# Pairing the output products of two slices beside attention, and moving a small load to another queue

## The chip, the core and the metric

The kernel runs on one core of a Trainium2 chip. The metric is the device time of one execution in microseconds (us). The core has a matmul engine (TensorE, PE; its weight loads appear as PEld), three engines for elementwise work (VectorE, DVE; ScalarE, ACT; GpSimd, POOL), SyncE (SP), which here only issues DMA transfers, and 16 DMA engines. PE writes its products to PSUM; DVE and ACT take them from there.

## What is computed

The reference, cut to what matters:

```python
# q, k, v: (4, 8, 576, 64); phi: (4, 8, 576, 32)
a = exp(phi - max(phi, axis=2)); a = a / (sum(a, axis=2) + 1e-9)
k_m, v_m = einsum('bhsm,bhsd->bhmd', a, k), einsum('bhsm,bhsd->bhmd', a, v)
attn = softmax(q @ k_m.T / sqrt(64))          # over 32 memory slots
x = (attn @ v_m).transpose(0, 2, 1, 3).reshape(2304, 512)
h = x @ w_in                                   # 512 -> 2048, weights in float64
x = (h * cos(h)) @ w_out                       # 2048 -> 512
p = domain_probs / (sum(domain_probs, -1) + 1e-9)
out = sum over 4 experts e of p[:, e] * (relu(x @ w1[e]) @ w2[e])   # 512 -> 1024 -> 512
```

## The kernel before

The kernel has three parts that overlap: attention, a first layer (h * cos(h)) and a second layer of four experts. Every fp32 product that has to be accurate is made of three matmuls on a high and a low half of both factors (`mm3`, L145 to L154; so nearly all matmuls have line L147), and the halves come from `split`: ACT writes the high half (L103), DVE or POOL the rest (L104).

**Attention** is eight parts, one for each of 4 batches and 2 groups of 4 heads. `attention` is a generator; a part is advanced by `next`. It loads phi, then k and v (two tiles of two heads, `kv`, three buffers) and q, all on SP's queue (L171, L178, L179, L182). The maximum `mx` (DVE, L189) goes through PE (`pt`, `bc`) and back (`bcs`), DVE subtracts (L201), ACT takes the Exp (L207). PE transposes q (`pq`, L214) and ACT copies it out (`qT`, L215). PE then forms `kvp` (L221), ACT scales it to `kvs` (L239), PE transposes that (`pkt`), DVE makes `kz` (L251) and `vz` (L257), and PE forms the scores `sc` (L271). DVE, POOL and ACT do the softmax (L278 to L293) and split the result into `attnT[b]`.

**The first layer** is worked in slices of 256 of the 2048 hidden columns (s = 0 to 7) for each batch b. A unit (s, b) has a projection, `vw = vz[b] x w_in slice` (`project`, L316: 16 matmuls into one PSUM buffer of pool `ps_o`, then a split into `vw`, two buffers), and, for each half `th` of the 576 rows, `hidden1` (12 matmuls `hp`, the h * cos(h) work and a split into `gt`, three buffers) and `output1` (L369): for each of four 128-row blocks d of the result, 6 matmuls into one PSUM bank `op`, and then a DVE instruction that copies the bank into the accumulator `acc` (slice 0, L384) or adds it (other slices, L386). Beside attention `op` takes its banks from `ps_o` alone, which has two buffers and which the projections use too; later it alternates between `ps_o` and `ps_a` (`wide`). `step1` works one unit: it calls `hidden1`, keeps up to two halves pending in `pend`, calls `output1` for the oldest one, and projects the next unit after the first half.

The order of the units is (0, 0), (1, 0), (0, 1), (1, 1), (0, 2), (1, 2), (0, 3), (1, 3) and then slice by slice over the batches. The first six are placed beside the attention parts 2 to 7, one unit for each part. The weights are float64 in memory; `narrow` (L122) loads them as `raw` and converts them with one ACT and three DVE instructions (L131, L132, L133, L136). The loads of the first slices' weights after the first one wait for a score Exp of attention on ACT's queue (`exps`, L285).

**The probabilities** are loaded and normalised by `load_probs` (L92): one transfer on POOL's queue, in pieces of 16 bytes (4 experts of one row), and four small DVE instructions.

The code is written in this order, but a scheduler reorders the instructions of each engine while the program is built; each engine then runs its own list strictly in order, and waits for others by semaphores. So what stands where is read from the built program.

Of the kernel before, what the change touches and what calls it, by code (L numbers as in the profile page):

```python
# [10 lines left out]
F32R = mybir.dt.float32r  # L11
# [13 lines left out]
def tile_kernel(  # L25
# [13 lines left out]
    nc = tc.nc  # L39
    B, H, S, D = q.shape  # L40
# [7 lines left out]
    TH = S // 2  # L48
    KD = DM // 128
    FS = 256  # L50
    NFC = FS // 128
    NS1 = DFF // FS
# [37 lines left out]
    p_all = const.tile([128, NT // 128, E], F32, name="p_all")  # L90

    def load_probs():  # L92
        nc.gpsimd.dma_start(out=p_all, in_=probs.rearrange("(i p) e -> p i e", p=128))
        p_sum = const.tile([128, NT // 128], F32, name="p_sum")
        nc.vector.tensor_reduce(out=p_sum, in_=p_all, axis=AX.X, op=ALU.add)
        nc.vector.tensor_scalar_add(p_sum, p_sum, 1e-9)
        nc.vector.reciprocal(out=p_sum, in_=p_sum)
        nc.vector.tensor_tensor(
            out=p_all, in0=p_all, in1=p_sum[:, :, None].to_broadcast([128, NT // 128, E]), op=ALU.mult
        )  # L100
# [44 lines left out]
    def mm3(ps, lt, rt, first, last, more=False):  # L145
        for i, (a, b) in enumerate(((0, 0), (0, 1), (1, 0))):
            nc.tensor.matmul(  # L147
                out=ps,
                lhsT=lt(a),
                rhs=rt(b),  # L150
                start=first and i == 0,
                stop=last and i == 2,
                skip_group_check=more,
            )  # L154
# [144 lines left out]
    wi = {}  # L299
    wo = {}  # L300
# [15 lines left out]
    def project(b, wi):  # L316
        vw_ps = ps_o.tile([128, 2, FS], F32, tag="o", name="vw_ps")
        for g in range(2):
            for i in range(HG):
                nc.tensor.matmul(  # L320
                    out=vw_ps[32 * i:32 * i + 32, g, :],
                    lhsT=vz[b][:, g, i, :],
                    rhs=wi[:, 2 * g + i // 2, :],
                    start=True,
                    stop=True,
                )
        vw = cs.tile([128, 2, 2, FS], F32R, tag="vw", name="vw")
        split(vw[:, 0], vw[:, 1], vw_ps)
        return vw

# [2 lines left out]
    def hidden1(b, th, vw):  # L333
        y_all = cs.tile([128, NFC, TH], F32, tag="y", name="y")
        kk_all = cs.tile([128, NFC, TH], F32, tag="kk", name="kk", bufs=1)
        gt = cs.tile([128, 2, NFC, TH], F32R, tag="g", name="gt", bufs=3)
        step = NFC if wide[0] else 1
        for f0 in range(0, NFC, step):
            hp = ps_h[0].tile([128, step, 512], F32, tag="h", name="hp")
            for i in range(step):  # L340
                fc = f0 + i
                for g in range(2):
                    mm3(
                        hp[:, i, :TH],
                        lambda x: vw[:, x, g, fc * 128:fc * 128 + 128],
                        lambda x: attnT[b][:, x, g, th * TH:th * TH + TH],
                        g == 0,
                        g == 1,
                    )
            hv = hp[:, :, :TH]  # L350
            y = y_all[:, f0:f0 + step]
            kk = kk_all[:, f0:f0 + step]
            marks.append(nc.scalar.activation(out=y, in_=hv, func=ACTF.Copy, scale=INV_2PI, bias=0.25))
            if wide[0]:
                nc.scalar.activation(out=kk, in_=y, func=ACTF.Copy, bias=ROUND)
                nc.vector.scalar_tensor_tensor(  # L356
                    out=y, in0=kk, scalar=ROUND, in1=y, op0=ALU.subtract, op1=ALU.subtract
                )
            else:
                nc.vector.tensor_scalar(  # L360
                    out=kk, in0=y, scalar1=ROUND, scalar2=ROUND, op0=ALU.add, op1=ALU.subtract
                )
                nc.gpsimd.tensor_tensor(out=y, in0=y, in1=kk, op=ALU.subtract)
            nc.scalar.activation(out=y, in_=y, func=ACTF.Sin, scale=-TWO_PI if wide[0] else TWO_PI)  # L364
            nc.vector.tensor_tensor(out=y, in0=hv, in1=y, op=ALU.mult)  # L365
            split(gt[:, 0, f0:f0 + step], gt[:, 1, f0:f0 + step], y, nc.gpsimd if wide[0] else nc.vector)
        return gt

    def output1(s, b, th, gt, wo):  # L369
        for d in range(KD):  # L370
            c = d % 2 if wide[0] else 0
            op = (ps_o, ps_a)[c].tile([128, 512], F32, tag="oa"[c], name="op")
            for fc in range(NFC):
                mm3(
                    op[:, :TH],
                    lambda x: wo[:, x, fc, d * 128:d * 128 + 128],
                    lambda x: gt[:, x, fc, :],
                    fc == 0,
                    fc == NFC - 1,
                )  # L380
            t0 = (b % 2) * S
            dst = x1v[:, b // 2, d, t0:t0 + S].rearrange("p (c u) -> p u c", u=2)[:, th]
            if s == 0:
                nc.vector.tensor_copy(out=dst, in_=op[:, :TH])  # L384
            else:
                nc.vector.tensor_tensor(out=dst, in0=op[:, :TH], in1=dst, op=ALU.add)  # L386

    vws = {}
    wide = [False]
    pend = []  # L390
    order = [(s, b) for b in range(B) for s in range(2)]
    order += [(s, b) for s in range(2, NS1) for b in range(B)]

    def project_next(n):
        if n + 1 < len(order):
            s2, b2 = order[n + 1]
            vws[n + 1] = project(b2, wi[s2])

    def step1(n):
        s, b = order[n]  # L400
        for th in range(2):
            if n > 8 and b in (1, 2) and s + 1 < NS1:
                (load_in, load_out)[b - 1](s + 1, marks[-1], th)
            pend.append((s, b, th, hidden1(b, th, vws[n]), wo[s]))
            if len(pend) > 2:
                output1(*pend.pop(0))
            if th == 0:
                project_next(n)

    parts = [attention(b, g) for b in range(B) for g in range(2)]  # L410
    np_ = len(parts)
# [13 lines left out]
        next(parts[i])  # L425
    load_in(1, exps[0])
    load_out(1, exps[1])
    nu = 0
    for n in range(2, np_):
        part = parts[n]  # L430
        if n + 2 < np_:
            next(parts[n + 2])
        if n + 1 < np_:
            next(parts[n + 1])
        if n + 2 < np_:
            next(parts[n + 2])
        next(part)
        next(part, None)
        if n <= 7:
            step1(nu)  # L440
            nu += 1
    wide[0] = True
    c_ctx.close()
    ps_h[0] = p_ctx.enter_context(tc.tile_pool(name="ps_h2", bufs=2, space=PSUM, reuse_waits="tile"))
    load_probs()
    at_ctx.close()
    wc = ctx.enter_context(tc.tile_pool(name="wc", bufs=2, side="right", reuse_waits="tile"))
    for n in range(nu, len(order)):
        s, b = order[n]
        if n == 6:  # L450
            load_in(2)
        if n == 8:
            load_out(2)
        step1(n)
    for p in pend:
        output1(*p)
    cs_ctx.close()

# [214 lines left out]
```

## Time and profile before

| | |
|---|---|
| three timed runs | 1221.29, 1222.03, 1224.94 us; median 1222.03 us |
| profiled execution | 1223.36 us, of which the span from the first to the last instruction is 1221.6 us |
| PE busy | 1181.9 us (97%), 7946 matmuls |
| DVE, ACT, POOL busy | 868.2, 485.6, 525.2 us |
| attention and the first six units | about 0 to 165 us |
| rest of the first layer | to about 454 us |
| second layer | about 454 us to the end |

All times of the trace count from the start of the span. Busy time is the union of an engine's instructions; matmuls overlap, so the share of a stretch in which PE is idle tells more than its busy share. The granted clock of PE has two levels in this trace, 1.0 (2.4 GHz) and 0.5 (1.2 GHz).

### The profile page before, as it was taken

How to read it: one execution, taken by the hardware profiler on the slowest of the kernel's cores; microseconds unless marked ns; L12 is line 12 of the kernel's file. 1: busy time of each engine (PE TensorE's matmuls, PEld its weight loads, DVE VectorE, ACT ScalarE, POOL GpSimd, SP SyncE). 2: the span in 40 equal slices, each digit the busy share in tenths (PEclk: the TensorE clock that was granted, in tenths of full speed). 3: DMA queues.
4: the chain of work that ended last, by engine and by line, in shares of the span. 5: the costliest groups of instructions: out<-in, count | busy, mean ns of one | idle time of the engine just before them, and what ended most of it. 6: DMA issues, size and time to landing. Idle time of an engine off the chain costs nothing.

```text
span 1221.6 us, 20025 instructions
## 1 busy us (share of the span) xinstructions
PE 1181.9 (97%) x7946; PEld 1050.3 (86%) x7946; DVE 868.2 (71%) x1571; ACT 485.6 (40%) x854; POOL 525.2 (43%) x609
## 2 busy tenths in 40 slices
PE   6788999999999999999999999999999999999998
PEld 5466788999999988888889898898889989888997
DVE  5798988798788788666666666678656665666665
ACT  2475755666566663232222223244222322322221
POOL 1443533332333852445445445546534544453420
PEclk8589999999999999999999999999999999999999
DMA  9953001112112110111111111113111111111102
GB/s 224 251 147 77 21 36 52 36 53 70 35 36 72 52 52 18 37 52 51 35 53 53 35 40 57 43 36 129 54 35 50 55 35 35 53 52 36 52 1 78
DMA packets 48062, 72.89 MB, mean 60 GB/s; under 512 B 2624, under 2 KB 31328, under 8 KB 47968
## 3 DMA queue, kind: packets, MB, share of 16 engines
q1 hardware_dynamic: 41024, 55.85, 16.1%
q10 hardware_dynamic: 6880, 15.73, 4.2%
q8 instruction: 62, 1.02, 0.3%
q14 instruction: 32, 0.26, 0.1%
q0 software_dynamic: 64, 0.04, 0.0%
HBM read 66.88 MB, written 4.72 MB: 59 GB/s over the span
## 4 chain that ended last, share of the span: by engine, by line
PE 62%; DVE 1%; issue 0%
PE op L147 33%; PE hp L147 29%; DVE x L485 1%; DVE sA L477 0%; DVE sB L498 0%; DVE acc L617 0%; DVE ht L582 0%; DVE u L558 0%; DVE acc L386 0%
## 5 line engine op out<-in xcount | busy, mean ns | idle before, releaser
L147 PE MATMUL op<-wb,ht 128*128 128x512 f32 x1728 | 439.3, 396 | 0.0
L147 PEld LDWEIGHTS hp<-x,wa 128*128 128x128 f32 x2688 | 380.3, 189 | 24.4 <-DVE x L485 3.6
L147 PE MATMUL hp<-x,wa 128*128 128x320 f32 (+1 forms) x2688 | 393.6, 295 | 3.2 <-DVE x L485 2.9
L147 PEld LDWEIGHTS op<-wb,ht 128*128 128x128 f32 x1728 | 312.7, 188 | 58.5
L617 DVE SCALAR_TENSOR_TENSOR acc<-op,p_all,acc 128x512 f32<-128x512 f32 x270 | 201.8, 748 | 137.7 <-PE op L147 137.4
L147 PE MATMUL op<-gt,wo 128*128 128x288 f32 x1536 | 228.8, 298 | 6.3 <-DVE acc L384 3.2
L147 PEld LDWEIGHTS op<-gt,wo 128*128 128x128 f32 x1536 | 211.7, 189 | 13.1 <-DVE acc L384 4.0
L111 POOL TENSOR_TENSOR wb<-raw,wb 128x256 fp32r<-128x256 f32 x124 | 89.5, 753 | 227.2 <-ACT wb L109 227.2
L588 ACT ACTIVATE ht<-c 128x256 fp32r<-128x256 f32 (+3 forms) x128 | 71.8, 562 | 283.5 <-DVE c L558 283.5
L104 POOL TENSOR_TENSOR gt<-y,gt 128x576 fp32r<-128x576 f32 x52 | 81.4, 1566 | 163.2 <-ACT gt L103 138.5
L589 DVE SCALAR_TENSOR_TENSOR ht<-c,ht 128x256 fp32r<-128x256 f32 (+3 forms) x128 | 93.7, 732 | 63.1 <-ACT ht L588 63.1
L147 PE MATMUL hp<-attnT,vw 128*128 128x288 f32 x768 | 129.6, 304 | 4.9 <-DVE y L365 3.8
L528 POOL TENSOR_TENSOR wa<-raw,wa 128x256 fp32r<-128x256 f32 x96 | 69.2, 748 | 149.1 <-ACT wa L518 149.1
L147 PEld LDWEIGHTS hp<-attnT,vw 128*128 128x128 f32 x768 | 109.6, 190 | 19.1 <-issue 14.3
L558 DVE TENSOR_TENSOR c<-hp,u 128x256 f32<-128x256 f32 (+1 forms) x192 | 87.3, 457 | 42.3 <-PE hp L147 37.9
L528 POOL TENSOR_TENSOR wa<-tt,wa 128x256 fp32r<-128x256 f32 x128 | 110.0, 889 | 0.0
L386 DVE TENSOR_TENSOR acc<-op,acc 128x288 f32<-128x288 f32 x224 | 96.5, 450 | 16.5 <-PE op L147 16.1
L565 ACT COPY p<-hp 128x256 f32<-128x256 f32 x64 | 25.7, 401 | 113.0 <-PE hp L147 113.0
L364 ACT ACTIVATE y<-y 128x576 f32<-128x576 f32 (+1 forms) x76 | 46.1, 609 | 61.3 <-DVE y L356 52.9
L103 ACT ACTIVATE gt<-y 128x576 fp32r<-128x576 f32 (+1 forms) x76 | 46.0, 605 | 37.6 <-DVE y L365 37.5
L518 ACT ACTIVATE wa<-raw 128x512 fp32r<-128x512 f32 x32 | 20.2, 632 | 85.5 <-PE hp L147 85.3
L365 DVE TENSOR_TENSOR y<-hp,y 128x576 f32<-128x576 f32 (+1 forms) x76 | 49.7, 655 | 5.2 <-ACT y L364 5.0
(101 smaller groups left out, 1062.4 us busy)
## 6 DMA issues: line engine op xcount, KB each, us to landing
raw<-in_moe_w_dram SPq DMA_DIRECT2D x60, 512.0 KB, 3.5
raw<-in_moe_w_out_dram ACTq DMA_DIRECT2D x14, 512.0 KB, 3.5
raw<-in_moe_w_in_dram ACTq DMA_DIRECT2D x12, 512.0 KB, 3.7
kv<-in_k_dram SPq DMA_DIRECT2D x16, 288.0 KB, 6.2
kv<-in_v_dram SPq DMA_DIRECT2D x16, 288.0 KB, 7.1
q<-in_q_dram SPq DMA_DIRECT2D x8, 576.0 KB, 9.2
out_dram<-acc SPq DMA_DIRECT2D x18, 256.0 KB, 2.0
phi<-in_phi_dram SPq DMA_DIRECT2D x8, 288.0 KB, 7.9
```

The lines of the kernel that those rows point to most:

```text
L103: nc.scalar.activation(out=hi, in_=src, func=ACTF.Copy)
L104: (eng or nc.vector).tensor_tensor(out=lo, in0=src, in1=f32(hi), op=ALU.subtract)
L111: (nc.vector if early and c % 512 else nc.gpsimd).tensor_tensor(out=t[:, 1, c:c + 256], in0=src[:, c:c + 256], in1=f32(t[:, 0, c:c + 256]) ...
L147: nc.tensor.matmul(out=ps, lhsT=lt(a), rhs=rt(b), start=first and i == 0, stop=last and i == 2, skip_group_check=more,)
L364: nc.scalar.activation(out=y, in_=y, func=ACTF.Sin, scale=-TWO_PI if wide[0] else TWO_PI)
L365: nc.vector.tensor_tensor(out=y, in0=hv, in1=y, op=ALU.mult)
L386: nc.vector.tensor_tensor(out=dst, in0=op[:, :TH], in1=dst, op=ALU.add)
L528: pool.tensor_tensor(out=wa[:, 1, o], in0=src, in1=f32(wa[:, 0, o]), op=ALU.subtract)
L558: nc.vector.tensor_tensor(out=out, in0=ps[:, :n], in1=sb, op=ALU.add)
L588: nc.scalar.activation(out=ht[:, 0, fc, lo:], in_=c[:, fc, lo:], func=ACTF.Relu)
L589: nc.vector.scalar_tensor_tensor(out=ht[:, 1, fc, lo:], in0=c[:, fc, lo:], scalar=0.0, in1=f32(ht[:, 0, fc, lo:]), op0=ALU.max, op1=ALU.su ...
L617: nc.vector.scalar_tensor_tensor(out=dst, in0=op, scalar=pe, in1=dst, op0=ALU.mult, op1=ALU.add)
```

## The change

Four things change. Slices 0 and 1 of a batch are grouped for the batches 1 to 3 (batch 0 keeps single units, as do all later slices). `output1` takes a list of units: for a pair it puts the 6 matmuls of slice 0 and the 6 of slice 1 of a block d into the same bank and evacuates it once, by a copy. A pair's output work is queued in two halves of two blocks each, after both units' `hidden1` of that row half; the projections of a pair are both made at one point. `step1` becomes the generator `layer1`, one `hidden1` for each `next`, two of them for each attention part. The `vw` tile gets a third buffer (4096 bytes in each partition) and `gt` a fourth (4608 bytes). The transfer of `load_probs` goes from POOL's queue to SP's. The program is built with `dynamic_dma_scratch_size=2048`.

```diff
     def load_probs():
-        nc.gpsimd.dma_start(out=p_all, in_=probs.rearrange("(i p) e -> p i e", p=128))
+        nc.sync.dma_start(out=p_all, in_=probs.rearrange("(i p) e -> p i e", p=128))
...
-        vw = cs.tile([128, 2, 2, FS], F32R, tag="vw", name="vw")
+        vw = cs.tile([128, 2, 2, FS], F32R, tag="vw", name="vw", bufs=3)
...
-        gt = cs.tile([128, 2, NFC, TH], F32R, tag="g", name="gt", bufs=3)
+        gt = cs.tile([128, 2, NFC, TH], F32R, tag="g", name="gt", bufs=4)
...
-    def output1(s, b, th, gt, wo):
-        for d in range(KD):
+    def output1(units, th, gts, ds):
+        b = units[0][1]
+        k = len(units)
+        for d in ds:
...
-            for fc in range(NFC):
-                mm3(
-                    op[:, :TH],
-                    lambda x: wo[:, x, fc, d * 128:d * 128 + 128],
-                    lambda x: gt[:, x, fc, :],
-                    fc == 0,
-                    fc == NFC - 1,
-                )
+            for j, (s, _) in enumerate(units):
+                for fc in range(NFC):
+                    mm3(
+                        op[:, :TH],
+                        lambda x: wo[s][:, x, fc, d * 128:d * 128 + 128],
+                        lambda x: gts[j][:, x, fc, :],
+                        j == 0 and fc == 0,
+                        j == k - 1 and fc == NFC - 1,
+                    )
...
-            if s == 0:
+            if units[0][0] == 0:
                 nc.vector.tensor_copy(out=dst, in_=op[:, :TH])
...
+    groups, n0 = [], 0
+    for n in [1, 1] + [2] * (B - 1) + [1] * ((NS1 - 2) * B):
+        groups.append(list(range(n0, n0 + n)))
+        n0 += n
+
+    def project_next(gi):
+        for n in groups[gi + 1] if gi + 1 < len(groups) else ():
+            s, b = order[n]
+            vws[n] = project(b, wi[s])
+
+    def layer1():
+        for gi, group in enumerate(groups):
+            pair = len(group) == 2
+            for th in range(2):
+                gts = []
+                for k, n in enumerate(group):
+                    s, b = order[n]
...
+                    gts.append(hidden1(b, th, vws[n]))
+                    units = [order[i] for i in group]
+                    if not pair:
+                        queue.append((units, th, gts, range(KD)))
+                    elif k == 1:
+                        queue.extend((units, th, gts, ds) for ds in (range(0, 2), range(2, 4)))
+                    if len(queue) + (pair and k == 0) > 2:
+                        output1(*queue.pop(0))
+                    if (th, k) == (int(pair), 0):
+                        project_next(gi)
+                    yield
...
         if n <= 7:
-            step1(nu)
-            nu += 1
+            next(steps)
+            next(steps)
...
-    nc = _bacc.Bacc("TRN2", target_bir_lowering=False, num_devices=1)
+    nc = _bacc.Bacc("TRN2", target_bir_lowering=False, num_devices=1, dynamic_dma_scratch_size=2048)
```

What the scheduler makes of it is seen in the built programs. On SP's queue at the start (a line that begins with - stands only in the program before, with + only in the new one; `raw_387` is the second half of the first w_in slice, the rows below it are the loads of attention parts 1 to 3):

```order
 L128 DMA raw_387<-in_moe_w_in_dram 128x2x512
+L93 DMA p_all<-in_moe_domain_probs_dram 128x18x4
 L171 DMA phi<-in_phi_dram 96x4x192
 L182 DMA q<-in_q_dram 96x4x384
+L171 DMA phi<-in_phi_dram 96x4x192
 L178 DMA kv<-in_k_dram 96x2x384
 L179 DMA kv<-in_v_dram 96x2x384
 L178 DMA kv<-in_k_dram 96x2x384
 L179 DMA kv<-in_v_dram 96x2x384
-L171 DMA phi<-in_phi_dram 96x4x192
```

The probabilities come in behind the first weights, and the phi of part 3 has moved ahead of the second k and v of part 1 and the first of part 2.

On DVE at the start, around `kz` of part 0 (`raw_381` and `raw_387` are the two halves of the first w_in slice on their way into `wi`):

```order
+L133 SCALAR_TENSOR_TENSOR raw_381<-raw_381 128x512
+L132 TENSOR_SCALAR raw_387<-raw_387 128x512
+L136 SCALAR_TENSOR_TENSOR wi<-raw_381 128x512
+L95 TENSOR_REDUCE p_sum<-p_all 128x18
+L133 SCALAR_TENSOR_TENSOR raw_387<-raw_387 128x512
 L251 TENSOR_TENSOR kz<-pkt,half 128x256
 L257 TENSOR_TENSOR vz<-pkt,mask 128x128
-L133 SCALAR_TENSOR_TENSOR raw_381<-raw_381 128x512
-L132 TENSOR_SCALAR raw_387<-raw_387 128x512
 L189 TENSOR_REDUCE mx<-phi 96x128
```

Part of the weight conversion and the sum over the probabilities, which stood before the first `dg`, now stand ahead of `kz`. On ACT at the same place, before:

```order
L199 COPY bcs<-bc 96x128
L215 COPY qT<-pq 128x3x96
L207 ACTIVATE a<-a 96x768
L215 COPY qT<-pq 128x3x96
L199 COPY bcs<-bc 96x128
L215 COPY qT<-pq 128x3x96 x2
L207 ACTIVATE a<-a 96x768
L215 COPY qT<-pq 128x3x96
L239 ACTIVATE kvs<-kvp,rs 128x256
```

and in the new program:

```order
L199 COPY bcs<-bc 96x128
L215 COPY qT<-pq 128x3x96 x3
L207 ACTIVATE a<-a 96x768
L215 COPY qT<-pq 128x3x96
L199 COPY bcs<-bc 96x128
L207 ACTIVATE a<-a 96x768
L131 ACTIVATE raw_381<-raw_381 128x512
L215 COPY qT<-pq 128x3x96 x2
L131 ACTIVATE raw_387<-raw_387 128x512
L239 ACTIVATE kvs<-kvp,rs 128x256
```

The first Exp has three copies of qT ahead of it instead of one, and the first `kvs` has both weight conversions ahead of it.

On PE around the projections of batch 1, before (`vw_ps` is a projection, `sc` the scores of part 3):

```order
L147 MATMUL hp<-attnT,vw 128x288 x6
L320 MATMUL vw_ps<-wi,vz 32x256 x4
L147 MATMUL hp<-attnT,vw 128x288 x6
L147 MATMUL op<-gt,wo 128x288
L271 MATMUL sc<-qT,kz 32x288 x8
L320 MATMUL vw_ps<-wi,vz 32x256 x4
L147 MATMUL op<-gt,wo 128x288 x5
L197 MATMUL bc<-dg,ones 96x128
```

and in the new program:

```order
L147 MATMUL hp<-attnT,vw 128x288 x12
L320 MATMUL vw_ps<-wi,vz 32x256 x8
L271 MATMUL sc<-qT,kz 32x288 x8
L320 MATMUL vw_ps<-wi,vz 32x256 x8
L197 MATMUL bc<-dg,ones 96x128
```

Where one projection stood, in two pieces, two stand on both sides of the scores, and the first `op` comes later.

## Rows read from the trace of the kernel before

**Rows 1.** The page: busy us by engine; the DMA engines' share in 40 slices.

```profile
PE 1181.9 (97%) x7946; PEld 1050.3 (86%) x7946; DVE 868.2 (71%) x1571; ACT 485.6 (40%) x854; POOL 525.2 (43%) x609
DMA  9953001112112110111111111113111111111102
```

**Rows 2.** Stretches: length, busy PE, PEld, DVE, ACT, POOL; PE clock, DMA share, GB/s.

```profile
0.00:29.00 29.00, 17.98 (x160) 14.44 (x160) 17.03 (x38) 8.35 (x16) 2.57 (x8) 0.88 1.02 223
29.00:63.00 34.00, 24.33 (x201) 15.75 (x201) 26.94 (x59) 16.07 (x33) 15.36 (x17) 0.55 1.00 248
63.00:104.00 41.00, 33.97 (x318) 26.65 (x318) 38.60 (x80) 26.77 (x51) 17.87 (x18) 0.87 0.54 128
100.70:104.10 3.40, 3.40 (x34) 2.63 (x33) 3.40 (x8) 1.29 (x3) 0.99 (x1) 0.50 0.00 0
104.00:165.00 61.00, 57.35 (x530) 46.19 (x530) 53.88 (x121) 41.33 (x80) 29.56 (x28) 1.00 0.12 33
165.00:210.00 45.00, 44.28 (x353) 40.15 (x351) 35.82 (x68) 25.35 (x41) 12.04 (x10) 1.00 0.14 46
210.00:445.00 235.00, 234.69 (x1914) 218.51 (x1913) 195.11 (x358) 145.70 (x229) 101.52 (x84) 1.00 0.18 55
467.00:1221.60 754.60, 750.66 (x4364) 671.64 (x4362) 481.56 (x821) 209.89 (x387) 343.25 (x446) 1.00 0.15 47
```

**Rows 3.** PE in order of time: start, length, what, [idle before it and releaser].

```profile
29.72 2.78 PE L221 MATMUL kvp<-kv,a 96*32 96x128 f32 x44 [1.93 <-DMA kv<-in_v_dram]
54.63 1.08 PE L320 MATMUL vw_ps<-wi,vz 128*32 128x256 f32 x8 [4.68 <-DVE wi L136]
100.12 0.64 PE L147 MATMUL hp<-attnT,vw 128*128 128x288 f32 x3 [2.49 <-DVE y L365]
```

**Rows 4.** PE's waits, 90 to 215 us: us in all, times, longest.

```profile
PE hp L147 <- DVE y L365: 3.8, 2, 2.5
PE op L147 <- DVE vw L104: 2.5, 5, 1.0
PE pkt L247 <- ACT kvs L239: 0.6, 1, 0.6
PE vw_ps L320 <- DVE acc L386: 0.3, 1, 0.3
PE hp L147 <- DVE ssm L287: 0.2, 1, 0.2
```

**Rows 5.** Groups by line: count, busy us, mean ns of one, idle before.

```profile
L386 DVE TENSOR_TENSOR acc<-op,acc 128x288 f32<-128x288 f32 x224 | 96.5, 450 | 16.5 <-PE op L147 16.1
L104 DVE TENSOR_TENSOR vw<-vw_ps,vw 128x512 fp32r<-128x512 f32 x32 | 22.0, 686 | 15.5 <-ACT vw L103 15.5
L285 ACT ACT_TABLE_LOAD x3 | 3.8, 1283 | 0.1
```

**Rows 6.** DVE in order of time.

```profile
10.14 0.23 DVE L95 TENSOR_REDUCE p_sum<-p_all 128x18 f32<-128x72 f32 x1 [1.75 <-DMA p_all<-in_moe_domain_probs_dram]
22.63 0.41 DVE L251 TENSOR_TENSOR kz<-pkt,half 128x256 f32<-128x256 f32 x1
98.17 1.44 DVE L189 TENSOR_REDUCE mx<-phi 96x128 f32<-96x768 f32 x1 [1.97 <-DMA phi<-in_phi_dram]
```

**Rows 7.** ACT in order of time.

```profile
15.78 0.54 ACT L215 COPY qT<-pq 128x288 f32<-128x288 f32 x1 [4.40 <-PE pq L214]
21.21 0.47 ACT L239 ACTIVATE kvs<-kvp,rs 128x256 f32<-128x256 f32 x1
23.26 0.70 ACT L131 ACTIVATE raw<-raw 128x512 f32<-128x512 f32 x1 [0.20 <-DMA raw<-in_moe_w_in_dram]
```

**Rows 8.** DMA, 0 to 12, 1 to 3.2, 24 to 29 us: packets, MB, share.

```profile
q0 software_dynamic: 64, 0.04, 3.2%
...
q1 hardware_dynamic: 432, 0.32, 54.1%
...
q1 hardware_dynamic: 830, 1.18, 111.0%
```

More of the change, by code (lines that the diff above doesn't have):

```diff
@@ L389, in tile_kernel @@
     wide = [False]
-    pend = []
+    queue = []
     order = [(s, b) for b in range(B) for s in range(2)]
     order += [(s, b) for s in range(2, NS1) for b in range(B)]
[L394 to L408, printed above, removed]
+    groups, n0 = [], 0
[13 more added lines that the diff above has]
+                    s, b = order[n]
+                    if n > 8 and b in (1, 2) and s + 1 < NS1:
+                        (load_in, load_out)[b - 1](s + 1, marks[-1], th)
+                    gts.append(hidden1(b, th, vws[n]))
[9 more added lines that the diff above has]
+                    yield
     parts = [attention(b, g) for b in range(B) for g in range(2)]
@@ L427, in tile_kernel @@
     load_out(1, exps[1])
-    nu = 0
+    steps = layer1()
     for n in range(2, np_):
@@ L447, in tile_kernel @@
     wc = ctx.enter_context(tc.tile_pool(name="wc", bufs=2, side="right", reuse_waits="tile"))
[L448 to L455, printed above, removed]
+    load_in(2)
+    for _ in range(4):
+        next(steps)
+    load_out(2)
+    for _ in steps:
+        pass
+    for p in queue:
         output1(*p)
```

## Prediction

> **What bounds the kernel now.** I read the page first, then the table of stretches, then who the matmul engine PE waited for, and last the first 60 us in order of time. The page shows PE busy for 1181.9 of 1221.6 us and VectorE (DVE) for 868.2 [rows 1]: PE is the engine to look at, and what it loses, it loses early. The table says where. From 467 us to the end (the second expert layer) PE is busy for 750.7 of 754.6 us, and from 210 to 445 us (the rest of the first layer) for 234.7 of 235 [rows 2]. Nothing in these stretches can get shorter while the matmuls stay the same in number, and the change keeps every one. The loss lies ahead of 210 us: PE is idle for 11.0 us up to 29 us, 9.7 us up to 63, 7.0 us up to 104, 3.7 us up to 165 and 0.7 us up to 210 [rows 2]. The granted clock says the same: 0.88, 0.55 and 0.87 in the first three stretches, 1.00 afterwards, so PE also spends much of the first 104 us at 1.2 instead of 2.4 GHz.
>
> Two different things hold PE there. Up to 63 us it is the loads: the DMA engines are busy throughout, at 223 to 248 GB/s [rows 2], and the second attention part's products (kvp) start at 29.72 us because a piece of v lands then [rows 3]. From 63 to 165 us it is DVE, busy for 92.5 of 102 us: softmax, splits and evacuations all queue on it, in order. The waits that PE has after 90 us are for DVE, but for 0.6 us for ACT: 3.8 us for y (L365), 2.5 us in five waits for the split of vw (L104), which holds a PSUM buffer that op needs, and 0.5 us in small ones, 7.4 us in all [rows 4].
>
> **The change part by part.**
>
> *Products.* No matmul is added or removed. The paired units are (0, b) and (1, b) for b = 1, 2, 3. Each used to evacuate its 2 halves x 4 banks alone: 8 copies for slice 0, 8 adds for slice 1. Now the 12 matmuls of both go into one bank, and 8 copies are all. Three batches lose 8 adds each, 24 of the 224 at 450 ns [rows 5]: 10.8 us of DVE. Batches 1 and 2 lie beside attention, so 16 x 0.45 = 7.2 us leave the stretch in which DVE is the late engine; the other 3.6 us leave the saturated stretch, where PE waits for no one, and are worth nothing.
>
> What can 7.2 us of DVE give? Not more than PE loses there: 3.8 + 2.5 us of waits [rows 4], and up to 1.7 us because PE runs at half clock for 3.4 us behind the longest of them (100.7 to 104.1 us) [rows 2], together 8.0 us. I take half, 4 us: DVE is one of several links in these waits (the 2.49 us wait of hp that ends at 100.12 us [rows 3] follows 1.97 us in which DVE itself waited for phi [rows 6]), and counted off the order, PE's attention products stand behind as many layer products as before (168 op and 114 hp ahead of the last sc in both). A fewer-evacuations gain of nothing is one end. Below nothing there is this: the projections of a pair stand one behind the other and hold both ps_o buffers, which the op banks share. The longest wait behind one split took 1.0 us, the five together 2.5 us [rows 4]; a second split at 0.7 us [rows 5] behind each of three pairs costs up to 2.1 us more. So the pairing is worth -4 us, between -8 and +2.
>
> *More buffers.* A third vw and a fourth gt remove waits only; they issue nothing. Their worth is within the 8 us above.
>
> *ACT.* Two more table loads stand on ACT in the new order (16 against 14), at 1283 ns [rows 5]: 2.6 us. ACT is busy for 41.3 of the 61 us from 104 to 165 [rows 2], so most of it is hidden by PE's other products; I charge 0.5 us, from 0 to 2.6.
>
> *The probabilities' load.* It leaves the POOL queue, where DVE waited 1.8 us for it at 10.1 us [rows 6]; that wait cost nothing, as the first Exp on ACT stands behind qT, whose q lands only at 15 us [rows 7]. On SP it now stands behind the first weights and ahead of phi, in the stretch where the loads bind. Queued behind it: phi and q of part 2, phi of part 3 (moved up ahead of kv), then the k and v of part 1 that PE waits for at 29.72 us. What it delays them by is not shown in this trace. As software packets it took 64 packets and 3.2% of 16 engines in the first 12 us: 0.38 us of all of them [rows 8], which now falls away. On SP its 2304 pieces have 16 bytes each. Ends: if a piece costs by its bytes, 36.9 KB at 223 GB/s [rows 2] are 0.2 us; if it costs what a packet of 741 bytes does, 2.2 us x 16 x 54.1% / 432 = 44 ns [rows 8], then 2304 x 44 / 16 = 6.3 us. I take 2 us, nearer the low end: a packet of 1422 bytes took 5 us x 16 x 111% / 830 = 107 ns [rows 8], so the price falls at least as fast as the size, and a large share per packet doesn't show. The phi moved ahead is 288 KB, at 236 GB/s (1.18 MB in 5 us [rows 8]) 1.2 us. The k and v of part 1 so land 2 + 1.2 - 0.4 = 2.8 us later, between 1.0 and 7.1. Nothing gives this back: the DMA engines stay full to about 60 us [rows 1], and DVE is nearly full behind it.
>
> The Trainium skill speaks against this move: "DMA: Bandwidth & Descriptors", Specifications, wants at least 512 bytes in a transfer and says that smaller ones are read, modified and written. No run here shows a 16-byte piece. Were each charged as 512 bytes, 1.18 MB at the row's 236 GB/s would be an estimated 5.0 us, and my sum would come out 3 us later.
>
> *The order at the start.* The sum p_sum (L95) now stands on DVE ahead of the second half of the weight conversion and of kz, so kz waits for this load. On ACT the first Exp stands behind three qT copies instead of one, and kvs behind the conversion of raw_387, which landed at 23.26 us [rows 7]. Before, kz ran at 22.63 us [rows 6]. Now kvs is at 23.9 us at the earliest, where it was 21.21 [rows 7]; p_all lands some 2 us after raw_387, at 25.3 us; then come L133 and kz, at about 26: 3.4 us late. That is beside the 2.8 us, not on top: unit 0 needs both parts, and part 1 is the later one. I take 3 us for the start, between 1 and 8.
>
> *Sum.* The profiled execution took 1223.36 us (span 1221.6). 1223.4 + 3 - 4 + 0.5 = 1222.9 us. The median of the three timed runs is 1222.03, 1.3 us under the profiled one, so the forecast for a median is 1221.5 us: **no change that can be told**. (A measurement of this kernel tells about 0.3%, 3.7 us, from no change.)
>
> **The rivals.**
>
> *Pairing wins.* DVE is the only late engine from 90 to 210 us, the waits of [rows 4] go, and PE keeps its full clock: -6 to -8 us. The load on SP costs by its bytes: +1 us. That gives -5 to -7, some 1216 us. For it: DVE at 88 to 94% in [rows 2] from 63 to 165 us. Against it: the unchanged interleaving on PE, and that the longest wait began with a load.
>
> *The start costs more (slower).* Place: kz of part 0 on DVE, behind p_sum. If a piece costs the 44 ns of the smaller packet, p_all lands at 23.3 + 6.3 = 29.6 us and kz runs at 30.3 us, 7.7 us late; so does the first score Exp, which releases the next weight loads on ACT's queue, and through them the weights wi of slice 1, for which PE already waits 4.7 us at 54.63 us [rows 3]. Then +7.7 - 4 + 0.5 gives +4.2, some 1226 us; with a pairing worth 2, 1228. It decides from the point where the start costs over 7.2 us (3.7 + 4 - 0.5), or over 5.2 us with a pairing worth 2: kz is late by 1.4 us and the load's own time, so the load decides from 3.8 to 5.8 us, 26 to 40 ns a piece. For it: three separate delays on one chain. Against it: the packet prices above, and the 1.8 us that DVE no longer waits for p_all at 10 us.
>
> *That it doesn't do what it says* can be left out: the order has 24 evacuations fewer.
>
> **How the numbers follow.** No change to tell: 0.44, 1221.5 us (1218 to 1226). Pairing wins: 0.32, 1216 us, the far end 1214. Start costs more: 0.24, 1226 us, the far end 1228. The range of 8 in 10 leaves a tenth out on each side: 1214 to 1227. Faster by over 0.3% has 0.32, slower 0.24, within 0.44.
>
> **What would show each step.** Right: DVE's first layer adds are 200 instead of 224; the p_all transfer shows 2304 packets more under 512 bytes; kvp of part 1 starts at 32 to 33 us and unit 0's first hp some 3 us later than before; PE's waits from 90 to 215 us come to 3 or 4 us instead of 7.4; from 215 us both kernels run alike, shifted. Wrong: if kz of part 0 runs before 24 us or after 29, the price of the pieces is wrong; if PE waits on the split of vw for more than 4 us, the pair's two projections cost what I put at the end of the range; if the stretch from 210 to 445 us gets shorter, matmuls have become cheaper, which nothing here explains.

## The result, and the profile after

The changed kernel takes 1232.38 us (median of four runs, 1229.93 to 1235.04) against 1222.41 us for the kernel before in the same comparison: 1.0088 times as long, with a 95% interval of 1.0070 to 1.0106. It is slower by about 10.8 us, and the forecast (1221.5 us, at most 1227) was wrong. The profiled execution took 1232.52 us, with a span of 1230.7 us.

The table of stretches of the changed kernel, to set beside [rows 2] (length, busy us of PE, PEld, DVE, ACT and POOL, then PE's clock, DMA share, GB/s):

```profile
63.00:104.00 41.00, 34.45 (x341) 27.70 (x342) 38.34 (x82) 28.54 (x54) 18.45 (x17) 0.92 0.52 128
104.00:165.00 61.00, 56.27 (x484) 46.17 (x482) 47.35 (x103) 41.55 (x78) 27.68 (x27) 0.89 0.13 34
165.00:210.00 45.00, 43.18 (x336) 39.87 (x337) 29.76 (x55) 24.82 (x40) 11.33 (x9) 1.00 0.17 52
210.00:445.00 235.00, 230.13 (x1863) 212.07 (x1862) 197.94 (x347) 141.20 (x222) 95.18 (x82) 1.00 0.16 51
467.00:1230.70 763.70, 758.47 (x4403) 679.30 (x4403) 489.64 (x834) 212.40 (x392) 343.60 (x446) 1.00 0.15 47
```

Two rows are bad. From 104 to 165 us the clock is 0.89 where it was 1.00 in [rows 2]; and from 210 to 445 us, the stretch that I had called full, PE is busy for 230.1 us where it was 234.7, with 51 matmuls fewer.

A table worked out from the traces says when the time is lost. Each hidden product is first read by one ACT copy (y from hp, L353), so the start of the n-th of these copies tells how far the first layer has come. The row of before is its time in us; the others are the difference to it in us (minus is ahead of before). The labels are those of the experiments below. Each row is a single execution: sp_only, bufs_no_pairs and irregular_no_pairs have the same lists on PE, DVE and ACT up to 197 us and still lie 3.4 us apart at the 11th and the 15th copy, so small differences say little.

| kernel | 11th | 15th | 29th | 35th | 45th | 59th | 75th |
|---|---|---|---|---|---|---|---|
| before | 118.1 | 133.4 | 190.3 | 224.2 | 277.3 | 354.1 | 438.8 |
| changed kernel | -6.3 | +0.8 | -0.1 | +4.9 | +5.7 | +8.9 | +8.6 |
| sp_only | +1.0 | +1.0 | +0.9 | -0.6 | -0.4 | -0.6 | -0.6 |
| bufs_no_pairs | -0.4 | -0.4 | -1.3 | -2.8 | -2.6 | -2.5 | -2.4 |
| pairs_of_1_and_2 | -5.5 | +1.7 | +0.7 | -0.3 | -0.2 | -0.2 | -0.2 |
| last_chunk_whole | -6.2 | +1.1 | -1.3 | -0.4 | -0.4 | -0.5 | -0.5 |
| irregular_no_pairs | +3.0 | +3.0 | +2.2 | +2.2 | +6.3 | +9.8 | +16.6 |
| two_exps_later | -5.5 | -3.6 | -3.9 | -5.4 | -5.2 | -5.2 | -5.3 |
| two_exps_later_all_pairs | -5.1 | -4.4 | -3.8 | +1.5 | +2.0 | +5.0 | +4.9 |

So the changed kernel was ahead, by 6.3 us at the 11th copy. That is progress and not only another order of the work: it has started 793 matmuls by then, the kernel before 802 by its own 11th copy, and nine matmuls are about 1 us. Within the next 15 us the lead was lost again, and from 190 us on another 9 us went.

**The first loss** is on ACT. In order of time (start, length, what):

```profile
114.60 1.28 ACT L207 ACT_TABLE_LOAD   x1
115.90 0.85 ACT L207 ACTIVATE a<-a 96x768 f32<-96x768 f32 x1
116.76 1.28 ACT L364 ACT_TABLE_LOAD   x1
118.06 0.44 ACT L364 ACTIVATE y<-y 128x288 f32<-128x288 f32 x1
...
119.48 1.28 ACT L285 ACT_TABLE_LOAD   x1
120.78 0.68 ACT L285 ACTIVATE st<-st 128x576 f32<-128x576 f32 x1
...
121.94 1.28 ACT L364 ACT_TABLE_LOAD   x1
123.23 0.44 ACT L364 ACTIVATE y<-y 128x288 f32<-128x288 f32 x1
```

Exp (L207), Sin (L364), Exp (L285), Sin again: four table loads of 1.28 us in 9 us, two of them ahead of each Sin of one half. In the kernel before, one load at 122.08 us serves both Exps. Both Sins come late, and both times PE stands. Its waits from 104 to 135 us (us in all, times, longest):

```profile
PE hp L147 <- DVE y L365: 3.0, 2, 1.9
```

And PE's clock falls behind the first of the two. The same columns as the table of stretches, in steps of 3 us:

```profile
117.00:120.00 3.00, 1.94 (x20) 1.61 (x19) 0.96 (x3) 2.88 (x5) 1.17 (x2) 0.95 0.41 121
120.00:123.00 3.00, 2.30 (x11) 1.94 (x9) 2.18 (x3) 2.97 (x4) 0.00 (x0) 0.50 0.27 75
123.00:126.00 3.00, 1.78 (x7) 1.78 (x8) 1.89 (x6) 2.03 (x6) 1.48 (x2) 0.50 0.00 0
126.00:129.00 3.00, 3.00 (x32) 2.14 (x31) 1.89 (x5) 1.53 (x5) 1.45 (x2) 0.50 0.00 0
...
132.00:135.00 3.00, 3.00 (x35) 1.76 (x32) 0.69 (x2) 0.65 (x2) 0.00 (x0) 0.77 0.02 5
```

The granted clock is 0.50 (1.2 GHz) from 119.7 to 133.4 us, while DVE, which had been the late engine, is idle for a quarter to three quarters of the time.

**The second loss** is the order of PE's own instructions. In the stage behind attention the kernel before repeats one pattern for nearly every unit. The rows of it are from last_chunk_whole, which has the same pattern (PE in order of time, x is the number of matmuls):

```profile
236.80 0.96 PE L147 MATMUL hp<-attnT,vw 128*128 128x288 f32 x6
237.69 1.07 PE L320 MATMUL vw_ps<-wi,vz 128*32 128x256 f32 x16
238.69 1.06 PE L147 MATMUL hp<-attnT,vw 128*128 128x288 f32 x6
239.59 2.56 PE L147 MATMUL op<-gt,wo 128*128 128x288 f32 x18
241.99 0.43 PE L147 MATMUL hp<-attnT,vw 128*128 128x288 f32 x2
242.26 0.95 PE L147 MATMUL op<-gt,wo 128*128 128x288 f32 x6
243.04 1.48 PE L147 MATMUL hp<-attnT,vw 128*128 128x288 f32 x10
```

The projection has hidden products on both sides, and no wait is marked. In the changed kernel the output products stand right behind the projection, another row of them follows two hidden ones later, and PE waits for DVE's add (in brackets: idle before it and the releaser):

```profile
207.85 1.07 PE L320 MATMUL vw_ps<-wi,vz 128*32 128x256 f32 x16 [0.66 <-DVE acc L389]
208.85 2.66 PE L147 MATMUL op<-gt,wo 128*128 128x288 f32 x18
211.35 0.43 PE L147 MATMUL hp<-attnT,vw 128*128 128x288 f32 x2
213.42 1.86 PE L147 MATMUL op<-gt,wo 128*128 128x288 f32 x12 [1.64 <-DVE acc L389]
```

DVE at that time:

```profile
211.08 1.92 DVE L136 SCALAR_TENSOR_TENSOR wi<-raw 128x512 uint32<-128x512 uint32 x1
212.92 0.45 DVE L389 TENSOR_TENSOR acc<-op,acc 128x288 f32<-128x288 f32 x1
```

The add that would free the bank needs 0.45 us, but stands behind a weight conversion of 1.92 us. The changed kernel's order of PE stays like this for some 16 units and is back in the old pattern by about 387 us. Its last wait ends at 361 us, and from there the table above stops growing. The waits marked from 180 to 440 us come to 6.1 us; counted from start to start, PE's gaps above the usual 0.13 us between two matmuls are 8.3 us more from the 29th to the 75th copy than in the kernel before, of the 8.7 us that it loses there.

### The profile page after: what moved, and what is told of

Read it like the earlier page. It is cut to its first block, busy times and chain, and to the rows that moved or that the text cites. A ratio compares the mean times of both kernels' runs of the same rounds, so it can differ in the third digit from the quotient of the medians.

```text
span 1230.7 us, 19976 instructions
## 1 busy us (share of the span) xinstructions
PE 1185.9 (96%) x7946; PEld 1055.7 (86%) x7946; DVE 868.2 (71%) x1547; ACT 487.7 (40%) x856; POOL 520.6 (42%) x608
## 4 chain that ended last, share of the span: by engine, by line
PE 82%; DVE 8%; DMA 4%; ACT 2%; issue 2%; POOL 1%; SPq 1%; ACTq 0%; POOLq 0%; DVEq 0%
PE op L147 43%; PE hp L147 34%; PE vw_ps L320 2%; PE kvp L221 1%; DMA phi<-in_phi_dram 1%; DMA raw<-in_moe_w_in_dram 1%; DVE y L356 1%; DVE acc L389 1%; DMA q<-in_q_dram 1%; DVE x L501 1%; DVE wi L136 1%; DMA kv<-in_v_dram 1%; DVE y L365 1%; DMA raw<-in_moe_w_out_dram 1%; DVE raw L133 1%
## 5 line engine op out<-in xcount | busy, mean ns | idle before, releaser
L147 PE MATMUL hp<-x,wa 128*128 128x256 f32 (+1 forms) x2688 | 393.8, 296 | 3.7 <-DVE x L501 2.9
L147 PE MATMUL op<-gt,wo 128*128 128x288 f32 x1536 | 235.5, 301 | 10.1 <-DVE acc L387 3.8
L104 POOL TENSOR_TENSOR gt<-y,gt 128x576 fp32r<-128x576 f32 x52 | 78.9, 1518 | 168.4 <-ACT gt L103 122.2
L389 DVE TENSOR_TENSOR acc<-op,acc 128x288 f32<-128x288 f32 x200 | 86.8, 449 | 19.7 <-PE op L147 19.1
L364 ACT ACTIVATE y<-y 128x576 f32<-128x576 f32 (+1 forms) x76 | 46.0, 607 | 50.7 <-DVE y L356 45.1
L356 DVE SCALAR_TENSOR_TENSOR y<-kk,y 128x576 f32<-128x576 f32 x52 | 48.8, 938 | 15.1 <-ACT kk L355 14.6
L365 DVE TENSOR_TENSOR y<-hp,y 128x576 f32<-128x576 f32 (+1 forms) x76 | 49.7, 654 | 10.8 <-ACT y L364 10.2
```

Of the source, the lines that this page charges most:

```text
L104: (eng or nc.vector).tensor_tensor(out=lo, in0=src, in1=f32(hi), op=ALU.subtract)
L147: nc.tensor.matmul(out=ps, lhsT=lt(a), rhs=rt(b), start=first and i == 0, stop=last and i == 2, skip_group_check=more,)
L356: nc.vector.scalar_tensor_tensor(out=y, in0=kk, scalar=ROUND, in1=y, op0=ALU.subtract, op1=ALU.subtract)
```

## The experiments

All were timed against the kernel before. Ratios have their 95% interval; below 1 is faster. A difference between two of these ratios is uncertain by some 0.002, which is 2.5 us.

| label | median us | ratio to before |
|---|---|---|
| sp_only | 1220.04 | 0.9980 [0.9970, 0.9990] |
| bufs_no_pairs | 1219.91 | 0.9986 [0.9973, 1.0000] |
| pairs_of_1_and_2 | 1220.66 | 0.9997 [0.9982, 1.0012] |
| last_chunk_whole | 1221.88 | 0.9994 [0.9983, 1.0006] |
| irregular_no_pairs | 1237.53 | 1.0124 [1.0089, 1.0159] |
| sin_after_exp_no_pairs | 1225.52 | 1.0026 [1.0011, 1.0041] |
| sin_after_exp_pairs | 1230.06 | 1.0064 [1.0038, 1.0091] |
| two_exps_later | 1218.14 | 0.9966 [0.9952, 0.9980] |
| two_exps_later_no_pairs | 1227.83 | 1.0050 [1.0035, 1.0065] |
| two_exps_later_pair_1 | 1219.98 | 0.9989 [0.9976, 1.0002] |
| two_exps_later_all_pairs | 1227.56 | 1.0045 [1.0031, 1.0059] |
| three_exps_later | 1221.18 | 0.9999 [0.9984, 1.0013] |

**First set: which part of the change costs.** Theories: the order that the pairs leave behind in the wide stage; the two more buffers; the half clock; the start.

sp_only, the kernel before with

```
-        nc.gpsimd.dma_start(out=p_all, ...)
+        nc.sync.dma_start(out=p_all, ...)
```

and the small scratch:

> The kernel before with one part of the change alone: the router probabilities go out through SP, with the small scratch. Pairs and extra buffers are left out. The order in the wide stage (from about 180 us on) is that of before. Order theory (the loss of the changed kernel is the irregular order of TensorE in the wide stage, which the pairs leave behind): no loss here, 1221 to 1224 us. Buffer theory (fourth gt and third vw let the queues of POOL, ACT and DVE drift): 1221 to 1224 us. Start theory (the 2304 pieces of 16 bytes on SP's queue cost at the start, my own +2 us): 1224 to 1226 us.

It is faster by 0.2% (2.4 us by the ratio), better than each theory had it. The move to SP, for which I had charged 2 us, is no loss. The trace shows 0.6 us of the gain by 439 us; the profiled execution took 1222.78 us, the longest of its twelve, so where the rest lies it doesn't show.

bufs_no_pairs, which adds `bufs=3` for vw and `bufs=4` for gt:

> As sp_only, with the third vw and the fourth gt buffer as well; every engine's order is the same as in sp_only. Order theory: within 1.5 us of sp_only. Buffer theory: the loss of the changed kernel appears, 1228 to 1232 us. Half-clock theory (the changed kernel loses because TensorE is granted 1.2 GHz at 119.7 to 133.4 us, which pairs bring about): as before, 1221 to 1224 us.

As fast as sp_only, with every engine's list unchanged: the buffers alone cost nothing and bring nothing. The buffer theory falls.

pairs_of_1_and_2, the changed kernel with

```
-    for n in [1, 1] + [2] * (B - 1) + [1] * ((NS1 - 2) * B):
+    for n in [1, 1, 2, 2] + [1] * (NS1 * B - 6):
```

> The changed kernel with batch 3 not paired: batches 1 and 2 stay paired, so attention stage and start are as in the changed kernel up to about 165 us, and the wide stage falls at once into the regular order of before (projection, 2 hidden, 18 output, 2 hidden, 6 output, 10 hidden, 24 output, 10 hidden). Order theory: the 9 to 10 us that the changed kernel loses from 195 us on are gone, 1221 to 1225 us. Buffer theory: 1229 to 1233 us. Half-clock theory: the stretch at 1.2 GHz is still there and so is the loss, 1229 to 1233 us.

A little under the expected band, and the changed kernel's loss is gone, although the stretch at 1.2 GHz is still there (its clock from 104 to 165 us is 0.89 as well, and it goes from -5.5 to +1.7 us between the 11th and the 15th copy). So the half clock isn't the 10 us.

last_chunk_whole, the changed kernel with all three pairs and one difference, the last item of the queue:

```
-   queue.extend((units, th, gts, ds) for ds in (range(0, 2), range(2, 4)))
+   queue.extend((units, th, gts, ds) for ds in ((range(KD),) if gi == 4 and th else (range(0, 2), range(2, 4))))
```

> The changed kernel with all three pairs, but the output products of the very last half of pair 3 are queued as one item of four banks and not as two of two. The order on every engine is the changed kernel's until about 195 us, then the regular order of before from the third unit on. Order theory: 1223 to 1227 us (the units until then still lose up to 4 us of the 9). Buffer and half-clock theories: unchanged against the changed kernel, 1230 to 1234 us.

Better than expected: 1.0088 has become 0.9994, 11.5 us. The same matmuls, evacuations, buffers and loads, and a PE order that differs only from the end of the last pair on (from 187 us; the lists of DVE, ACT and POOL differ from 188, 189 and 200 us). The order is what costs; none of these 11.5 us can come from what both kernels have in common, the half clock included.

**Second set: the order without pairs, and the table loads.** irregular_no_pairs has no pair at all; only the last half of unit (1, 3) is queued in two items, which shifts the phase of all that follows:

```
-    for n in [1, 1] + [2] * (B - 1) + [1] * ((NS1 - 2) * B):
+    for n in [1] * (NS1 * B):
...
-                        queue.append((units, th, gts, range(KD)))
+                        queue.extend((units, th, gts, ds) for ds in ((range(0, 2), range(2, 4)) if n == 7 and th else (range(KD),)))
```

> The changed kernel without any pair, except that the output products of the last half of unit (1,3) are queued as two items of two banks. TensorE's order up to about 180 us is that of bufs_no_pairs; from there it stays irregular for some 20 units of the wide stage (the changed kernel: some 16). Order theory: loses as the changed kernel does, 0.3 to 0.6 us a unit, 1226 to 1232 us, with TensorE waiting for DVE's adds into acc. If the loss needs the pairs: 1219 to 1222 us, as bufs_no_pairs.

It loses more than expected: 1.0124 against 0.9986 for bufs_no_pairs, 16.9 us. Its order stays irregular to the end of the layer, and the table shows it losing all the way, from +2.2 us at the 35th copy to +16.6 at the 75th. PE's waits from 180 to 440 us, first of this kernel, then of bufs_no_pairs:

```profile
PE op L147 <- DVE acc L389: 8.6, 10, 1.8
PE op L147 <- DVE vw L104: 0.8, 3, 0.3
```

```profile
PE op L147 <- POOL gt L104: 0.2, 1, 0.2
```

The changed kernel stands between them:

```profile
PE op L147 <- DVE acc L389: 2.8, 3, 1.6
PE op L147 <- DVE vw L104: 1.1, 4, 0.4
PE vw_ps L320 <- DVE acc L389: 0.7, 1, 0.7
```

Between 180 and 455 us irregular_no_pairs has 16 idle times of PE of over 0.1 us. All lie behind a projection and 8 to 25 output products, with no row of five or more hidden products between, and eleven of them end with an add into acc: there PE asks for banks faster than DVE gives them back. Such a row alone is not enough: last_chunk_whole has one (projection, 18 output, 2 hidden, 6 output) at 205.8 us and loses 0.15 us in it. Whether the number of banks in a row or the conversions ahead of the add count more isn't separated by these runs; that the order costs is shown, this mechanism inside it is read from the traces.

For the first loss the theory was that with fewer table loads ahead of those Sins PE stands less, and the half clock goes. sin_after_exp_no_pairs and sin_after_exp_pairs hold every Sin beside attention behind the Exp of the scores that was written last:

```
+            with tc.issue_after(exps[-1].ins) if not wide[0] else nullcontext():
                 nc.scalar.activation(out=y, in_=y, func=ACTF.Sin, ...)
```

> As bufs_no_pairs, with one more rule beside attention: a Sin of ACT stands behind the Exp of the scores that was written last before it, which leaves 12 table loads (14 in bufs_no_pairs); the wide stage falls into the regular order. Table theory (a pair's gain of 6 us at 118 us is lost again to Exp and Sin taking turns on ACT at 115 to 123 us): little to win here, 1216 to 1221 us. Rival, that the first Sin now waits too long: 1221 to 1226 us.

> As pairs_of_1_and_2, with the same rule for Sin behind Exp: 12 table loads in place of 16, no two Sins of one half parted by an Exp. Table theory: the stretch at 1.2 GHz at about 120 to 133 us goes, and with it 5 to 8 us: 1213 to 1217 us. Rival (the granted clock falls there for another reason, or the Sin waits for a late Exp): 1218 to 1224 us.

Both are slower, although they have 12 table loads in place of 14 and 16: the first lies in the range of the rival, the second above both ranges. The rule was too wide: it also holds the first Sins, which now stand behind an Exp that comes late. The first load of their table starts at 72.2 and 72.6 us (62.4 before), and the third copy of the table above is 10.3 and 10.7 us late. So fewer loads alone don't make the kernel faster.

two_exps_later is pairs_of_1_and_2 with only the two Exps held that stand at the bad place and after it (`sins` collects the Sins):

```
+        with tc.issue_after(sins[-1].ins) if 2 * b + g == 7 else nullcontext():
             nc.scalar.activation(out=a, in_=a, func=ACTF.Exp)
...
+            with tc.issue_after(sins[-1].ins) if 2 * b + g == 6 else nullcontext():
                 exps.append(nc.scalar.activation(out=st, in_=st, func=ACTF.Exp))
```

> As pairs_of_1_and_2, with two Exps alone held back behind the Sin written last (the Exp of phi of part 7 and the Exp of the scores of part 6): 14 table loads, and those at 115 to 123 us are two in place of four. Table theory: 1214 to 1218 us. Rival: 1218 to 1224 us.

It has the lowest median of all, 1218.14 us, at the border of the two ranges. It is faster than both kernels by more than the measurement's uncertainty, but 0.9966 can't be told from the 0.9980 of sp_only. Two of the four loads are gone at the bad place. The first Sin (L368 here) runs at 117.07 us without a load ahead of it, in pairs_of_1_and_2 at 118.91; an Exp (L288 here) still parts it from the second (ACT in order of time):

```profile
117.07 0.44 ACT L368 ACTIVATE y<-y 128x288 f32<-128x288 f32 x1 [1.60 <-POOL y L366]
...
118.50 1.28 ACT L288 ACT_TABLE_LOAD   x1
```

PE still stands once, for 2.4 us, but the half clock lasts only 3.4 us, from 123.4 to 126.9 us (steps of 3 us, as above):

```profile
120.00:123.00 3.00, 0.84 (x7) 0.60 (x5) 1.12 (x3) 2.97 (x6) 0.00 (x0) 1.00 0.51 161
123.00:126.00 3.00, 2.79 (x12) 2.77 (x13) 1.89 (x8) 1.78 (x5) 2.13 (x2) 0.57 0.00 0
126.00:129.00 3.00, 3.00 (x37) 1.60 (x37) 2.88 (x8) 1.60 (x4) 0.86 (x2) 0.86 0.00 0
```

Between the 11th and the 15th copy it falls back by 5.5 - 3.6 = 1.9 us, where pairs_of_1_and_2 falls back by 7.2. The clock is the larger part of that: PE's waits for y from 104 to 135 us are 3.0 us in pairs_of_1_and_2 and 2.4 us here, the time at 1.2 GHz is 13.7 us there and 3.4 us here. By an estimate, 10.3 us more at half the clock cost some 5 us.

**Third set: do the two causes add up, and is it the pairs?** The same rule with no pairs, with one pair, with all three, and with one Exp more:

> The control of two_exps_later: the same two Exps held behind the Sin written last, but no pairs (bufs_no_pairs with that rule), wide stage in the regular order. If two_exps_later is faster because of its pairs: 1219 to 1222 us here, as bufs_no_pairs or a little above. If the two Exps alone bring the gain: 1216 to 1219 us, as two_exps_later.

> As two_exps_later with batch 1 alone paired; regular order in the wide stage. If each pair gives about half of what two_exps_later gains on bufs_no_pairs (2 us): 1218.5 to 1220 us. If all of it lies at the first pair, where the table loads were: 1217.5 to 1219 us.

> The changed kernel with all three pairs and the two Exps held; its wide stage stays irregular for some 15 units, as in the changed kernel. If the two causes add up, the attention stage is as in two_exps_later (no stretch of 13 us at 1.2 GHz) and the wide stage loses 8 to 10 us with TensorE waiting for the adds into acc: 1225 to 1230 us. If the half clock brought about the rest too, the wide stage loses nothing: 1217 to 1220 us.

> As two_exps_later with the Exp of the scores of part 5 held as well: 14 table loads, regular order in the wide stage. If a held Exp costs nothing while TensorE has output products to do: 1216 to 1219 us. If attention is now late behind it: 1220 to 1224 us.

All pairs: 1227.56 us, as expected if the causes add up. Against the changed kernel the ratio goes from 1.0088 to 1.0045, 5.3 us, for the Exps alone; against two_exps_later it is 1.0045 to 0.9966, 9.7 us, for the third pair and the order that it leaves in the wide stage. The table shows where: 3.8 us ahead at the 29th copy, as two_exps_later is (3.9), and 4.9 us behind at the 75th.

One pair: 1219.98 us, as the guess "half for each pair" had it, though it can't be told from bufs_no_pairs. No pairs: 1227.83 us, above all that I expected; it is 4.7 us behind the kernel before at the 75th copy. Without pairs holding the same two Exps costs 7.8 us (0.9986 to 1.0050), so this is no clean control, and what the pairs are worth by themselves stays open. Three Exps: 1221.18 us, in the range for a late attention; the third costs 3 us (4 by the ratios).

## Why the prediction was wrong

**The stretch that was full.** The step that failed is "Nothing in these stretches can get shorter", from which I went on to "from 215 us both kernels run alike, shifted". True, it couldn't get shorter; but it could get longer, and it had no place in my sum or in a rival. PE at 234.7 of 235 us in [rows 2] belongs to one pattern of the order, not to the work. The scheduler writes that pattern anew from the state of the queue of output work behind attention: one item of that queue, split or whole, decides it. From 210 to 445 us, where I had put nothing, PE now waits for adds into acc, and from the 29th to the 75th copy the changed kernel falls back by 8.7 us. Measured for the order: 11.5 us (last_chunk_whole against the changed kernel), 9.7 us (third set, with the third pair), and 16.9 us in a kernel without pairs.

**ACT's two more table loads.** I charged 0.5 us, 2.6 at most, since ACT had room in 104 to 165 us. Holding two Exps back, which takes two loads away, was worth 5.3 us (all pairs) and 3.8 us (pairs 1 and 2, 0.9997 to 0.9966); it moves the Exps as well, so this is not the price of the loads alone. The share of busy time was the wrong view: the loads stand ahead of the two Sins of one half, and hp waits for those. And I gave this term no price for the clock, although I had done so for the pairing, where [rows 2] shows 3.4 us at 1.2 GHz behind such a wait; here it was 13.7 us. The Trainium skill has the rule for it ("ScalarE: Activation LUTs", Rules for kernel authors): group functions by their table, and do all of one before the next. The trace agrees where the grouping costs no wait (two_exps_later), and disagrees where it does (sin_after_exp_no_pairs: two loads fewer than bufs_no_pairs and 4.9 us more).

**The products.** I said -4 us, between -8 and +2. At the 11th copy the kernels with pairs are 5 to 6 us ahead wherever the Exps and Sins up to there stand as in the changed kernel, so a gain of that size is there. In three_exps_later and sin_after_exp_pairs, where they don't, it is 1.7 and 2.5 us, and sin_after_exp_no_pairs is 3.4 us ahead without any pair. That the gain comes from DVE's evacuations, as I had it, no run separates. What the pairs are worth at the end depends on the rest: against bufs_no_pairs (0.9986), pairs 1 and 2 lose 1.3 us with the table loads (0.9997), which can't be told from nothing, and gain 2.4 us without (0.9966), which barely can. The third pair, whose 8 adds I had put at nothing, is worth nothing where its last output work is queued whole (0.9994, last_chunk_whole); queued in two items, it brings the irregular order. DVE's adds are 200, as I said:

```profile
L389 DVE TENSOR_TENSOR acc<-op,acc 128x288 f32<-128x288 f32 x200 | 86.8, 449 | 19.7 <-PE op L147 19.1
```

**The start.** I charged 3 us, between 1 and 8, and made a rival of it. Nothing of it shows in the time. Of the changed kernel, SP's issue of the load and of the phi behind it, kz, the second part's products and unit 0's first hidden product:

```profile
9.05 0.37 SPq L93 DMA_DIRECT2D p_all<-in_moe_domain_probs_dram  x1
11.39 8.50 SPq L171 DMA_DIRECT2D phi<-in_phi_dram  x1
```

```profile
24.94 0.41 DVE L251 TENSOR_TENSOR kz<-pkt,half 128x256 f32<-128x256 f32 x1
...
29.98 2.77 PE L221 MATMUL kvp<-kv,a 96*32 96x128 f32 x44 [1.48 <-DMA kv<-in_v_dram]
...
40.57 0.78 PE L147 MATMUL hp<-attnT,vw 128*128 128x288 f32 x4
```

kz is 2.3 us later than in [rows 6], where I had said 3.4; the first layer starts no later for it. The products of part 1 start at 29.98 us, 0.3 us later than in [rows 3] and not 2.8, and unit 0's first hidden product is as early as before. The packet records of the trace give 9.1 ns for each piece, 1.3 us of all 16 engines: more than the bytes alone (0.2 us), less than the 2 us that I took. So a price that falls as fast as the size, which I read from two larger packets, did not hold down to 16 bytes (44 ns for 741 bytes); that the k and v are still only 0.3 us late, where I had added up 2.8, the traces leave open. The Trainium skill names 512 bytes as the least for the full rate ("DMA: Bandwidth & Descriptors", Specifications). The trace agrees that 16 bytes don't reach it, 28 GB/s in these 1.3 us, but my estimate of 5.0 us from that rule was nearly four times too high. The page of the profile counts

```profile
DMA packets 50317, 72.88 MB, mean 59 GB/s; under 512 B 4912, under 2 KB 33584, under 8 KB 50224
```

2288 small packets more than before (2624), and sp_only, which has as many, is faster.

**PE's waits from 90 to 215 us** did not fall from 7.4 us [rows 4] to 3 or 4, they rose to 11.3. Four of the seven rows:

```profile
PE hp L147 <- DVE y L365: 3.7, 4, 1.9
PE op L147 <- DVE acc L389: 1.6, 1, 1.6
PE bc L197 <- DVE dg L195: 1.6, 1, 1.6
PE op L147 <- DVE vw L104: 1.5, 1, 1.5
```

The wait for y is as long as before (3.8 us): behind y stands the Sin on ACT. The wait for the split of vw fell by 1.0 us. New are the waits for copies and adds into acc, 3.4 us in all, most of them from 200 us on, and the one for dg.

## What to carry to other kernels

When a scheduler orders the instructions, a stretch without a wait is a property of its order: compare the built orders of the stretches behind the edit too, row by row, before calling them unchanged, and look for long rows of products that need evacuation right behind a projection, with little other work between. A table load is to be judged by who waits for the function behind it, not by how busy the engine is. A kernel that gains in one place and loses in another should be taken apart by small edits that move one order at a time; the fastest here was two pairs with two Exps held back, though one line of the change, the load on SP, can't be told from it.

## What the hardware did that I had not expected

- 2304 pieces of 16 bytes, read in one transfer on SP's queue while the DMA engines were full, did not make the kernel slower (sp_only 0.9980), though each took 9.1 ns in the trace, the transfer took 13.5 us from issue to landing and SP's next issue took 8.50 us (0.33 in the kernel before).
- Idle times of PE of like length had quite different prices. In the changed kernel PE idled for 1.1 us to 119.04 us; the granted clock fell to 0.50 at 119.7 us and stayed there to 133.4, through a second idle time of 1.9 us and then 9 us in which PE was busy throughout. In two_exps_later PE was busy for only 0.84 of the 3 us from 120, and the clock was at 0.50 for 3.4 us only, to 126.9 us. In the kernel before, 2.49 us of idle time [rows 3] were followed by 3.4 us at half clock [rows 2]. And sp_only and bufs_no_pairs, whose lists are the same on every engine, show 10.2 us at half clock (97.6 to 107.9) behind an idle time of 2.32 us, and 3.4 us (101.4 to 104.8) behind one of 2.15 us.
- A change of table on ACT took 1.28 us, and nothing more shows: an Exp ended at 116.75 us, the load ran from 116.76 to 118.04, and the Sin began at 118.06.
